# Hash-masked attention and a SiLU feed-forward: one batch's attention interleaved by hand with the feed-forward of the batch before, scores stationary, silu through tanh

## Chip, cores and metric

One core of one Trainium2 chip. The metric is device time in microseconds (us), median of several executions. Every profile is of a run in the fast state, and ratios use fast runs alone. A few single runs were in the slower state (longer, at a lower clock).

Engines are named as in the profile: PE is TensorE matmul, PEld its weight loads, ACT ScalarE, DVE VectorE, POOL GpSimd, SP SyncE, which issues transfers. "av" stands for the product of the exp'd scores with the values.

## The reference, cut to what matters

```python
# q, k, v: (4 batches, 8 heads, 768, 64);  proj: (64, 6)
q_bits = (einsum('bhsd,dk->bhsk', q, proj) > 0)          # 6 hash bits a row; the same for k
mask   = q_bucket[:, :, :, None] == k_bucket[:, :, None, :]
scores = where(mask, q @ k.T / 8, -1e9)
attn   = softmax(scores);  x = (attn @ v) -> (3072, 512)  # 8 heads side by side
h = x @ w_in                                             # (512, 2048)
out = (h * sigmoid(h)) @ w_out                           # (2048, 512), fp32
```

Both kernels put the mask into the matmul: each row carries its six bits as +-0.5 beside its 64 values. A pair of rows whose bits all agree gets the largest bit product, and any disagreement pushes exp down to nothing. Both compute the bits' products in fp32, because only their signs count.

## The kernel before

Attention for all 32 heads first, the feed-forward for all tokens last. One head, cut:

```python
for b in range(B):
    for h in range(H):
        # ... loads of q_sb, k_sb, v
        for t in range(NJ): nc.tensor.transpose(tq_ps[0:64, ...], q_sb[:, t, :], ident)   # L132, fp32
        for t in range(NJ): nc.tensor.transpose(tk_ps[0:64, ...], k_sb[:, t, :], ident)   # L135
        nc.vector.tensor_copy(out=qT32, in_=tq_ps[0:64, :])                               # L140
        nc.vector.tensor_copy(out=kT32, in_=tk_ps[0:64, :])                               # L142
        nc.scalar.mul(QT[0:64, :], qT32, QS); nc.scalar.copy(KT[0:64, :], kT32)
        # bits: fp32 projection into 6 partitions, compare, for k (L151, L153) and q (L158, L160)
        # sum of v by six matmuls (L167)
        for jt in range(NJ):
            # scores: keys stationary, 768 queries moving                                  # L179, L181
            nc.scalar.activation(out=ut, in_=st_ps, func=AF.Exp, bias=ebias, scale=ESC)    # L184
        for jt in range(NJ):
            # values and ones stationary, 768 columns of exp'd scores moving               # L194
            nc.tensor.matmul(o_ps[:, c0:c1], VV[:, jt, :], u[jt][:, c0:c1], ...)
        # copies out (L197, L199), a transfer of the sums to other partitions;
        # per two heads four reciprocals of 128x192 (L94) and two products (L100)
# then: weights cast on GpSimd, and for each 512 tokens
nc.scalar.activation(out=gt, in_=h_ps, func=AF.Sigmoid)                                    # L237
nc.vector.tensor_tensor(out=gt, in0=gt, in1=h_ps, op=ALU.mult)                             # L238
```

The softmax here doesn't subtract the row's maximum and nothing guards it: scores larger than these inputs give would overflow.

## Time and profile before

| | before |
|---|---|
| time, median of the first 3 runs | 676.81 us (675.65 to 682.14) |
| attention, up to the first feed-forward matmul | 502 us |
| feed-forward, with nothing beside it | 178 us |
| mean granted clock of TensorE, 20 to 485 us | 0.74 |
| the same, 515 to 680 us | 1.00 |
| PE, DVE, ACT busy in the span | 86%, 51%, 43% |

Read the two clocks together with the busy shares. Work at clock 0.5 takes twice as long and the engine still reads as busy. So 86% busy is not 86% of what PE can do.

### The profile page before, as it was taken

The numbers are of one execution on the slowest core, as the hardware profiler recorded it, in microseconds if no ns is written. First come the engines' busy times: TensorE is split into PE (matmuls) and PEld (weight loads), VectorE is DVE, ScalarE is ACT, GpSimd is POOL, SyncE is SP. The second block draws the span as 40 slices with busy tenths as digits, with TensorE's granted clock in tenths as the row PEclk, the third lists the DMA queues.
The fourth block names the chain that finished last, engine by engine and source line by source line (L and its number), as shares of the span: only waits on it lengthen the run. The fifth ranks groups of instructions, "written<-read, shape, count | busy, mean of one in ns | idle before, by whom it ended". The sixth has DMA issues, their size and how long they took to land.

```text
span 680.6 us, 6388 instructions
## 1 busy us (share of the span) xinstructions
PE 581.9 (86%) x2432; PEld 249.7 (37%) x2432; DVE 344.8 (51%) x363; ACT 294.3 (43%) x338; POOL 45.6 (7%) x60
## 2 busy tenths in 40 slices
PE   6997977878797977878797977979798999999996
PEld 2342433333343424333333423333333444444442
DVE  2254637384645537363754548263638345254451
ACT  2654444454455544444464545444463224133140
POOL 4422000000000000000000000000000000000000
PEclk9876767597777769676877869676779999999999
DMA  9754224042222224142222224030100100101101
GB/s 267 217 149 87 41 41 70 17 76 41 42 40 41 40 41 69 32 64 31 50 40 41 40 41 81 20 39 7 23 13 15 47 31 32 62 16 47 46 16 63
DMA packets 84271, 37.12 MB, mean 55 GB/s; under 512 B 76560, under 2 KB 76560, under 8 KB 83728
## 3 DMA queue, kind: packets, MB, share of 16 engines
q1 hardware_dynamic: 34064, 27.27, 14.3%
q0 software_dynamic: 25088, 3.15, 7.2%
q10 hardware_dynamic: 25088, 6.29, 4.5%
q8 instruction: 19, 0.31, 0.2%
q14 instruction: 12, 0.10, 0.0%
HBM read 27.26 MB, written 6.29 MB: 49 GB/s over the span
## 4 chain that ended last, share of the span: by engine, by line
PE 76%; DVE 20%; issue 3%; DMA 1%; ACT 0%; SPq 0%; DVEq 0%
PE o_ps L194 13%; PE st_ps L179 12%; PE o_ps L243 12%; PE h_ps L232 11%; PE tk_ps L151 9%; PE st_ps L181 5%; DVE KT L153 5%; DVE xT L100 4%; DVE qT L140 4%; PE tq_ps L158 4%; PE tq_ps L132 4%; DVE numpair L197 3%; PE o_ps L190 3%; DVE kT L142 2%; DVE spair L94 1%
## 5 line engine op out<-in xcount | busy, mean ns | idle before, releaser
L184 ACT ACTIVATE u<-st_ps,ebias 128x768 f16<-128x768 f32 x192 | 163.8, 901 | 141.7 <-PE st_ps L181 141.7
L179 PE MATMUL st_ps<-QT,KT 70*128 70x512 f16 x192 | 108.3, 569 | 29.8 <-DVE KT L153 29.8
L140 DVE COPY qT<-tq_ps 64x768 f32<-64x768 f32 x32 | 30.4, 950 | 142.2 <-PE tq_ps L132 141.7
L237 ACT ACTIVATE g<-h_ps 128x1024 f16<-128x1024 f32 x48 | 49.1, 1023 | 107.5 <-PE h_ps L232 107.5
L232 PE MATMUL h_ps<-xT,win 128*128 128x512 f16 x384 | 87.5, 380 | 2.6 <-DVE g L238 2.6
L243 PE MATMUL o_ps<-wout,g 128*128 128x512 f16 x384 | 87.2, 379 | 2.3 <-DVE osb L248 2.3
L94 DVE RECIPROCAL spair<-spair 128x192 f32<-128x192 f32 x64 | 79.8, 1309 | 2.2 <-DMA spair<-stmp 1.8
L181 PE MATMUL st_ps<-QT,KT 70*128 70x256 f16 x192 | 74.5, 388 | 0.0
L238 DVE TENSOR_TENSOR g<-g,h_ps 128x1024 f16<-128x1024 f16 x48 | 58.4, 1220 | 31.1 <-ACT g L237 31.1
L158 PE MATMUL tq_ps<-qT,proj 64*6 64x256 f32 (+1 forms) x128 | 51.9, 531 | 24.7 <-DVE qT L140 22.8
L151 PE MATMUL tk_ps<-kT,proj 64*6 64x256 f32 (+1 forms) x128 | 65.8, 650 | 7.6 <-DVE kT L142 7.6
L194 PE MATMUL o_ps<-u,VVo 128*128 128x512 f16 x192 | 66.5, 459 | 0.0
L147 ACT ACTIVATE QT<-qT 64x768 f16<-64x768 f32 x32 | 27.0, 842 | 75.6 <-DVE qT L140 75.6
L179 PEld LDWEIGHTS <-KT 70*128 70x128 f16 x192 | 24.1, 126 | 95.8 <-issue 92.4
L194 PE MATMUL o_ps<-u,VVe 128*128 128x512 f16 x192 | 56.4, 393 | 0.0
L243 PEld LDWEIGHTS <-g 128*128 128x128 f16 x384 | 37.3, 97 | 49.7 <-issue 6.2
L232 PEld LDWEIGHTS <-win 128*128 128x128 f16 x384 | 37.7, 98 | 48.1 <-issue 3.5
L197 DVE COPY numpair<-o_ps 64x768 f32<-64x768 f32 x32 | 30.6, 955 | 44.2 <-PE o_ps L194 43.7
L153 DVE TENSOR_SCALAR KT<-tk_ps 6x768 f16<-6x768 f32 x32 | 30.6, 955 | 34.1 <-PE tk_ps L151 34.1
L248 DVE COPY osb<-o_ps 128x512 f32<-128x512 f32 x24 | 16.6, 692 | 59.0 <-PE o_ps L243 59.0
L132 PE MATMUL tq_ps<-ident,q_sb 128*64 128x128 f32 x192 | 37.1, 311 | 5.6 <-DMA q_sb<-in_q_dram 5.6
L199 ACT COPY stmp<-o_ps 64x768 f32<-64x768 f32 x32 | 25.3, 792 | 35.7 <-DVE numpair L197 35.1
(35 smaller groups left out, 404.3 us busy)
## 6 DMA issues: line engine op xcount, KB each, us to landing
k_sb<-in_k_dram ACTq DMA_DIRECT2D x32, 192.0 KB, 3.5
q_sb<-in_q_dram SPq DMA_DIRECT2D x32, 192.0 KB, 2.6
spair<-stmp SPq DMA_DIRECT2D x32, 192.0 KB, 2.9
out_dram<-osb SPq DMA_DIRECT2D x24, 256.0 KB, 2.0
win<-in_moe_w_in_dram SPq DMA_DIRECT2D x4, 1024.0 KB, 6.7
wout<-in_moe_w_out_dram SPq DMA_DIRECT2D x16, 256.0 KB, 3.5
VVe<-in_v_dram POOLq DMA_DIRECT2D x16, 96.0 KB, 4.5
VVo<-in_v_dram POOLq DMA_DIRECT2D x16, 96.0 KB, 4.1
```

Of the source, the lines that this page charges most:

```text
L94: nc.vector.reciprocal(out=spair[:, c0:c1], in_=spair[:, c0:c1])
L132: nc.tensor.transpose(tq_ps[0:64, t * P : (t + 1) * P], q_sb[:, t, :], ident)
L151: nc.tensor.matmul(tk_ps[64:70, c0:c1], proj32, kT32[:, c0:c1], start=True, stop=True)
L153: nc.vector.tensor_scalar(out=KT[64:70, :], in0=tk_ps[64:70, :], scalar1=0.0, scalar2=0.5, op0=ALU.is_ge, op1=ALU.subtract)
L158: nc.tensor.matmul(tq_ps[64:70, c0:c1], proj32, qT32[:, c0:c1], start=True, stop=True)
L179: nc.tensor.matmul(st_ps[:, 0:512], kslice, QT[:, 0:512], start=True, stop=True)
L181: nc.tensor.matmul(st_ps[:, 512:S], kslice, QT[:, 512:S], start=True, stop=True)
L184: nc.scalar.activation(out=ut, in_=st_ps, func=AF.Exp, bias=ebias, scale=ESC)
L194: nc.tensor.matmul(o_ps[:, c0:c1], VV[:, jt, :], u[jt][:, c0:c1], start=False, stop=(jt == NJ - 1))
L232: nc.tensor.matmul(h_ps[:, c, :], w_in16[dt][:, ft * P : (ft + 1) * P], xT[dt][:, t0 : t0 + TCH], start=(dt == 0), stop=(dt == NDT - 1))
L238: nc.vector.tensor_tensor(out=gt, in0=gt, in1=h_ps, op=ALU.mult)
L243: nc.tensor.matmul(o2_ps, g_tiles[ft // 2][:, ft % 2, tt * P : (tt + 1) * P], w_out16[ft], start=(ft == 0), stop=(ft == NFT - 1))
```

## The change

Four intents: fill PE's gaps in attention with the feed-forward of the batch before; cut PE work in attention by giving each matmul more to do; take the long VectorE operations out of each head's chain; and keep one activation table loaded.

- **Order by hand.** Instructions are issued in program order. One step is one block of 128 keys of one head (192 steps); feed-forward units are handed out evenly over a batch's 48 steps.
- **Heads in pairs.** One fp32 transpose turns two heads; one projection with a block-diagonal 128x32 weight gives both heads' bits; four such projections write four groups of 32 partitions.
- **Exp'd scores stationary.** Each output has tokens on partitions and 65 columns (64 values and the sum), so normalising is a reciprocal of six elements and one product. x must then be transposed.
- **silu as h(1 + tanh(h/2))**, with the factor 0.5 taken at the output.
- **Weights** are cast while they are loaded, at the start, on the GpSimd queue.

The core of the diff, cut:

```diff
-            for t in range(NJ):
-                nc.tensor.transpose(tq_ps[0:64, t * P : (t + 1) * P], q_sb[:, t, :],
-                                    ident)
+            nc.tensor.transpose(tp[:, j * P : (j + 1) * P],
+                                src[:, t].rearrange("p h d -> p (h d)"), ident)
...
+        for c in range(4):
+            p, n = 2 * Q + c // 2, c % 2
+            nc.tensor.matmul(bp[32 * c : 32 * c + 32, 0 : c1 - c0], pw,
+                             qk32[p][:, n * S + c0 : n * S + c1],
+                             start=True, stop=True)
...
-                    nc.tensor.matmul(o_ps[:, c0:c1], VV[:, jt, :], u[jt][:, c0:c1],
-                                     start=False, stop=(jt == NJ - 1))
+        for t in range(NJ):
+            nc.tensor.matmul(o_ps[h][:, t, :], u[:, t * P : (t + 1) * P], vv[:, jt, :],
+                             start=False, stop=True,
+                             skip_group_check=True)
...
-            nc.scalar.activation(out=gt, in_=h_ps, func=AF.Sigmoid)
-            nc.vector.tensor_tensor(out=gt, in0=gt, in1=h_ps, op=ALU.mult)
+            nc.scalar.activation(out=th, in_=hp, func=AF.Tanh, scale=0.5)
+            nc.vector.scalar_tensor_tensor(out=g[ci][:, grp * f : (grp + 1) * f, :],
+                                           in0=th, scalar=1.0, in1=hp,
+                                           op0=ALU.add, op1=ALU.mult)
...
+    for s in range(NSTEP):
+        for fn in at.pop(s, []):       # transposes, casts, projections, loads planned for this step
+            fn()
+        if s % 48 == 3 and s > 48:
+            moeq.extend(moe_units(s // 48 - 1))
+        # n = units left / steps left in this batch, rounded up
+        for _ in range(n):
+            moeq.popleft()()
+        av(s)
+        if s + 2 < NSTEP:
+            score(s + 2)
```

## The prediction

> **What bounds the kernel now.** I read the busy times first, then the slices, then three stretches, then the waits and one head in order of time.
>
> ```profile
> span 680.6 us, 6388 instructions
> PE 581.9 (86%) x2432; PEld 249.7 (37%) x2432; DVE 344.8 (51%) x363; ACT 294.3 (43%) x338; POOL 45.6 (7%) x60
> PE   6997977878797977878797977979798999999996
> ...
> PEclk9876767597777769676877869676779999999999
> ```
>
> TensorE is busy 86% of the span. The slices show two regimes: about 29 slices at 6 to 9 tenths with a granted clock wandering between 0.5 and 0.9, then 11 at 9 tenths and a clock of 0.9 or more. The stretches put numbers on them (columns: the stretch, its length, busy us and count of PE, PEld, DVE, ACT, POOL, then mean granted clock, DMA share, GB/s):
>
> ```profile
> 20.00:485.00 465.00, 386.29 (x1573) 164.06 (x1572) 250.58 (x268) 229.27 (x273) 37.26 (x48) 0.74 0.30 53
> 485.00:515.00 30.00, 25.93 (x109) 11.33 (x108) 15.33 (x16) 15.75 (x17) 0.00 (x0) 0.81 0.06 14
> 515.00:680.00 165.00, 156.50 (x716) 69.56 (x713) 74.00 (x72) 42.97 (x42) 0.00 (x0) 1.00 0.11 39
> ```
>
> The first 502 us are attention: the first feed-forward matmul (L232) starts at 502.4. Less the first 15.6 us, in which the first scores are prepared, that is (502 - 16) / 32 = 15.2 us a head. The feed-forward is the last 178 us, at clock 1.00 and with nothing else beside it. In attention no engine is full; each head is a chain PE, VectorE, PE, VectorE with the clock halved for most of it:
>
> ```profile
> 211.60 1.45 PE tq_ps L158 x4
> 213.06 2.51 PE tk_ps L151 x4
> 215.57 0.02 issue
> 215.59 0.97 DVE KT L153
> 216.56 0.14 issue
> 216.69 0.58 PE st_ps L179
> 217.28 0.21 PE st_ps L181
> ```
>
> So a copy out, a fp32 projection, a compare (0.97 us on six partitions) and only then scores. ScalarE waits for scores for 141.7 us in all (L184 behind L181). VectorE can be in the way too: four reciprocals took 4.99 us in one piece at 201.97, 79.8 us in all.
>
> **What the Trainium skill says.** (1) "TensorE: Matmul & The Clock Gate", Part 1, has the clock gate at full or half rate, set by recent activity of the array. The trace agrees: the granted clock is only ever 0.5 or 1.0, and averages 0.74 in attention and 1.00 in the feed-forward. (2) "Perfetto Trace Analysis", Optimization Strategy, advises interleaving regimes whose most-contended engine differs. The stretches fit: ACT is busy 49% in attention but 26% in the last 165 us, while PE goes from gaps to 95%. (3) "ScalarE: Activation LUTs", Table sets, puts exp and tanh in one set and sigmoid in another; before there are two table loads of 1283 ns. With exp and tanh alternating 96 times, sigmoid would cost a load at each switch; tanh costs none. (4) "TensorEngine Tiling (Array Packing)", Tiling Modes, has four 128x32 tiles that can run in parallel; the new projections write four 32-partition groups. No run here shows it.
>
> **The change, part by part.** First TensorE at full clock. Costs are start-to-start times from the order of events: 512 columns 0.2155 us, 256 columns 0.108, 128 columns with its own weight load 0.055 (six L167 took 0.50 us, of which the last is 0.22), one fp32 transpose 0.109 (four L132 added 0.44 to the chain), one fp32 projection of 768 columns 1.29 (four starts, 0.43 apart for the 512 half and 0.215 for the 256).
>
> - Transposes of q and k: heads go in pairs, so 384 become 192. 41.9 us to 20.9.
> - Projections: 64 of 768 columns become 32 (two heads in one, with a block-diagonal weight). 82.6 us to 41.3 if one after the other, 10.3 if the four column groups run side by side. I take 26.
> - Sums of v on PE (192 x 0.055 = 10.6) go to GpSimd.
> - Scores: the same 192 x 0.323 = 62.
> - Attention times values: before, u moved, 192 x 0.323 plus 32 delta rows of the same size, 72.4 us. Now u is stationary and 65 columns move: 1152 pairs of weight load and short matmul. Streaming 65 columns is about 27 ns; one timed weight load began 31 ns ahead of its matmul (L179 at 107.19 and 107.22). Their sum is 58, and 55 is the closest spacing measured. I take 0.055: 63.4 us, plus 32 delta matmuls of 390 columns, 5.2.
> - New transposes of x: 96 x 0.055 = 5.3.
> - Feed-forward: the same columns, 256 x 0.2155 + 256 x 0.108 + 384 x 0.2155 = 165.6, hence 41.4 a batch.
>
> Sum before: 41.9 + 82.6 + 10.6 + 62 + 72.4 + 165.5 = 435 us at full clock. After: 20.9 + 26 + 62 + 63.4 + 5.2 + 5.3 + 165.6 = 348. So 87 us of PE work go, but the larger gain is in the other 246 us of the 681: half clock and gaps of attention.
>
> ScalarE: exps start 0.78 us apart when back to back (three in 2.48 us, each 0.90). 192 x 0.78 = 150. A tanh of 512 is about 1.023 - 512 x 0.833 ns = 0.60 us (the sigmoid of 1024 took 1.023): 96 x 0.60 = 57. Copies of 512 out of PSUM, 0.58 by the same step from L199's 0.79: 48 x 0.58 = 28. In sum 235. VectorE: the product of 1024 took 1.22, so 512 takes about 0.69: 96 x 0.69 = 66; the 24 outputs 0.69 each, 17; copies of x 16 x 0.95 = 15; normalising 32 x 0.7 = 22 (reciprocals are now of six elements); bits about 9. In sum 129. GpSimd: casts of 1536 elements at the 0.92 ns of L213, 32 x 1.42 = 45, and some 40 for v. So PE is the bound wherever the feed-forward runs beside attention.
>
> Now the time, in four stages; one step is one block of 128 keys of one head, 192 in all.
>
> - Start, 28 us. Before, the first score came at 15.6. Now the loads are twice as large, two pairs need 24 transposes (at half clock 0.22 each, 5 us), six copies, then all projections (at half clock up to 10 us), bits, and row transfers of some 3 us before a score. Then the first step waits for pair 2's q, which is issued behind those transfers and shares bandwidth with 8.4 MB of weights.
> - First batch, 48 steps without feed-forward, 52 us. PE at full clock: 0.323 + 0.33 + 0.03 + 0.11 + 0.13 + 0.03 = 0.95; ACT 0.78 + 0.15 = 0.93. Two score buffers make a ring: exp ends, av and the next score (0.65), exp again (0.90), with about 0.3 of latencies, for two steps: 0.93. Three limits within 0.02 leave little room; I take 1.08.
> - Three batches with feed-forward, 144 steps, 274 us. PE 0.95 + 41.4/48 = 1.81 to 1.83. ACT in the half with tanh 0.93 + 0.60 = 1.53, in the other half 0.93. With 4% for waits 1.90.
> - Last feed-forward alone, 41.4, plus final normalising, transposes and out transfer of about 6: 48 us.
>
> 28 + 52 + 274 + 48 = 402 us.
>
> **The rivals.** (a) **The weight loads do not hide.** A 128-column weight load lasts 97 ns in the records; if each pair took 100 ns, 1152 x 0.045 = 52 us more: 454. Against it: the loads overlap in the trace, one begins 2 ns after its predecessor's matmul. If they hide entirely, the pair takes about 30 ns: 29 us less, 373. (b) **The clock stays halved.** At the clock of attention before, 0.74, the first batch's PE need is 1.3 a step (+11 us), and the interleaved steps would take 2.5 (+85 us): about 495. For it: short gaps in each step. Against it: the feed-forward stretch held 1.00 throughout at 95% busy, and the interleaved stage should be as dense. I expect at most the first batch to suffer. (c) **A PSUM ring becomes the bound.** Three one-bank buffers serve transposes, projections, both feed-forward products and x. A hidden block needs 0.87 on PE, a wait behind an exp (up to 0.8), tanh 0.6, product 0.69, perhaps 0.3 of latencies: 3.3 us, with two steps (3.7) until its buffer comes round, and less where a transpose unit takes a turn. If that binds in the tanh half, some 0.3 x 72 = 22 us more: 424. (d) **Projections in parallel or in series**: 16 us less or 15 more. (e) **The start** could take 10 us more behind the weights' transfer.
>
> **Range and chances.** The pair cost gives -29 to +52 with the low half likelier, projections +-15, the ring 0 to +22, clock 0 to +20. Not all go one way: 374 to 438. Even with (a) and (c) together, 476, it is far below 677. Slower would take an error of 270 us. Faster 0.985, same 0.01, slower 0.005.
>
> **What would show it.** In the changed profile: PE over 90% busy and granted clock near 1.0 in the stretches of batches 2 to 4; steps of about 1.9 us there; starts of the 65-column matmuls about 55 ns apart; four projection matmuls of a unit starting together or 0.43 us apart; one table load; VectorE near 130 us and ScalarE near 235. I am wrong in the mechanism if the interleaved steps show PE waiting for tanh's product or for an exp for more than 0.2 us each, if the clock there is below 0.95, or if the first 48 steps take more than 70 us.

## The result and the profile after

The changed kernel took 380.69 us (median of 4, 377.21 to 382.31), the kernel before 676.23. The ratio is 0.562 (95% interval 0.558 to 0.566).

The page of the changed kernel, busy times and slices:

```profile
span 378.8 us, 7151 instructions
PE 329.2 (87%) x2880; PEld 193.7 (51%) x2880; DVE 127.2 (34%) x241; ACT 230.1 (61%) x337; POOL 105.9 (28%) x174
...
PE   4540578988999999999999999999999999999995
...
PEclk9955689999999999999999999999999999999999
```

PE's busy share hardly moved, 86% to 87%; what it means did. From the eleventh slice to the last but one it is at 9 tenths, with the clock at full. Stretches of the changed kernel, cut where the stages begin (same columns as in the prediction):

```profile
0.00:26.00 26.00, 11.37 (x49) 6.75 (x49) 5.88 (x27) 6.31 (x9) 16.44 (x32) 0.84 0.52 126
26.00:92.00 66.00, 45.74 (x491) 26.60 (x489) 9.94 (x23) 42.45 (x60) 27.01 (x43) 0.83 0.72 151
92.00:330.00 238.00, 227.56 (x2102) 137.17 (x2103) 88.86 (x158) 167.03 (x245) 62.45 (x100) 1.00 0.23 64
330.00:379.00 49.00, 44.48 (x242) 23.15 (x240) 22.49 (x34) 14.33 (x24) 0.00 (x0) 1.00 0.10 38
```

Three interleaved batches take 238 us at 96% PE and clock 1.00. The weak stretch is the second: a first batch of 48 steps that takes 66 us, with DMA busy 72%.

Why an interleaved step is as short as it is, in TensorE's order of events:

```profile
151.35 0.34 PE L212 MATMUL o_ps<-vv,u 128*128 128x65 f16 x6
151.53 0.49 PE L195 MATMUL s_ps<-qka 71*128 71x512 f16 x2
151.86 1.03 PE L266 MATMUL o_ps<-wout,g 128*128 128x512 f16 x4
152.73 0.35 PE L212 MATMUL o_ps<-vv,u 128*128 128x65 f16 x6
152.91 0.49 PE L195 MATMUL s_ps<-qka 71*128 71x512 f16 x2
...
155.23 1.07 PE L168 MATMUL bp_ps<-qk,pw 128*32 128x512 f32 x8
```

Starts, not durations, tell the rate: one 65-column record lasts 0.19 us here, yet the next begins 0.03 us after it began. The six pairs of weight load and 65-column matmul occupy 151.35 to 151.53, 0.18 us; scores 0.33; four feed-forward matmuls 0.87. The sum is 1.38, and none of these lines carries a wait: PE is the bound, as predicted. In the whole stretch PE is idle for 10.4 us, and 9.7 of them are waits of the first matmul of a head for the normalising of the head before. The last line is a projection unit: eight records (fp32 takes two per matmul) in 1.07 us, where four in series would start 4 x 0.86 us of work. The first four of them start within 20 ns, which the prediction named as the sign that they run side by side.

And the first batch's two long waits, in the order of events of all engines (PE's idle time and what ended it stand in brackets):

```profile
22.68 2.38 POOL L120 DMA_DIRECT2D win<-in_moe_w_in_dram  x4
...
24.51 13.75 SPq L70 DMA_DIRECT2D k_sb<-in_k_dram  x1
...
38.73 0.69 PE L136 MATMUL tp_ps<-ident,k_sb 128*128 128x128 f32 x2 [9.83 <-DMA k_sb<-in_k_dram]
...
48.64 1.12 PE L136 MATMUL tp_ps<-ident,q_sb 128*128 128x128 f32 x4 [4.50 <-DMA q_sb<-in_q_dram]
```

The weights are issued at 22.68. A load of k issued just after holds the SP queue for 13.75 us, where an earlier one took 0.83, and PE stands still. These are steps 2 and 6 of the first batch, counted from 0 (the expectations below call the first of them step 1).

| stage | predicted us | measured us |
|---|---|---|
| start, to the first av | 28 | 26.3 |
| first batch, 48 steps | 52 | 66.0 |
| three interleaved batches, 144 steps | 274 | 238.0 |
| last feed-forward and end | 48 | 48.5 |
| sum | 402 | 378.8 (span) |

DVE was busy 127.2 us (129 predicted), ACT 230.1 (235), with one table load instead of two.

### The profile page after: what moved, and what is told of

It is laid out like the page before. It is cut to its first block, busy times and chain, and to the rows that moved or that the text cites. A ratio compares the mean times of both kernels' runs of the same rounds, so it can differ in the third digit from the quotient of the medians.

```text
span 378.8 us, 7151 instructions
## 1 busy us (share of the span) xinstructions
PE 329.2 (87%) x2880; PEld 193.7 (51%) x2880; DVE 127.2 (34%) x241; ACT 230.1 (61%) x337; POOL 105.9 (28%) x174
## 4 chain that ended last, share of the span: by engine, by line
PE 71%; DVE 9%; DMA 9%; ACT 5%; SPq 3%; issue 2%; POOL 0%; ACTq 0%; POOLq 0%
PE o_ps L266 21%; PE h_ps L249 20%; PE s_ps L195 12%; DMA k_sb<-in_k_dram 9%; PE o_ps L212 8%; PE bp_ps L168 4%; DVE x_pr L222 3%; PE tp_ps L136 3%; ACT u L197 3%; PE o_ps L208 2%; DVE g L255 2%; ACT th L253 2%; DVE osb L271 1%; PE xt_ps L232 1%; SPq L70 1%
## 5 line engine op out<-in xcount | busy, mean ns | idle before, releaser
L197 ACT ACTIVATE u<-s_ps 128x768 f16<-128x768 f32 x192 | 153.8, 813 | 74.7 <-PE s_ps L195 73.8
L249 PE MATMUL h_ps<-xT,win 128*128 128x512 f16 (+1 forms) x512 | 93.9, 326 | 0.3 <-DVE xT L234 0.3
L255 DVE SCALAR_TENSOR_TENSOR g<-th,h_ps 128x512 f16<-128x512 f32 x96 | 66.1, 688 | 58.2 <-ACT th L253 58.2
L212 PEld LDWEIGHTS <-u 128*128 128x128 f16 x1152 | 60.0, 99 | 40.7 <-ACT u L197 13.4
L143 POOL TENSOR_SCALAR qka<-qk 64x1536 f16<-64x1536 f32 x16 | 23.5, 1466 | 170.7 <-ACT qk L138 170.7
L212 PE MATMUL o_ps<-vv,u 128*128 128x65 f16 x1152 | 68.1, 196 | 3.5 <-ACT u L197 3.1
L253 ACT ACTIVATE th<-h_ps 128x512 f32<-128x512 f32 x96 | 57.3, 597 | 22.5 <-PE h_ps L249 20.1
L195 PE MATMUL s_ps<-qka 71*128 71x512 f16 x192 | 48.8, 337 | 4.3 <-POOL vsb L156 4.3
L195 PE MATMUL s_ps<-qkb 128*128 128x512 f16 x192 | 48.0, 332 | 0.0
L138 ACT COPY qk<-tp_ps 128x512 f32<-128x512 f32 x48 | 28.2, 587 | 26.7 <-PE tp_ps L136 26.7
L136 PE MATMUL tp_ps<-ident,k_sb 128*128 128x128 f32 x96 | 17.6, 302 | 10.5 <-DMA k_sb<-in_k_dram 10.4
L143 POOL TENSOR_SCALAR qkb<-qk 64x1536 f16<-64x1536 f32 x16 | 23.5, 1471 | 1.2
```

What stands on the lines that cost most here:

```text
L136: nc.tensor.transpose(tp[:, j * P : (j + 1) * P], src[:, t].rearrange("p h d -> p (h d)"), ident)
L138: nc.scalar.copy(qk32[p][:, 512 * i : 512 * (i + 1)], tp)
L143: nc.gpsimd.tensor_scalar(out=dst[rows, :], in0=qk32[p][rows, :], scalar1=CS, scalar2=1.0, op0=ALU.mult, op1=ALU.mult)
L195: nc.tensor.matmul(sp[:, c0:c1], ks, t[rows, c0:c1], start=True, stop=True)
L197: nc.scalar.activation(out=u, in_=sp, func=AF.Exp, scale=ESC)
L212: nc.tensor.matmul(o_ps[h][:, t, :], u[:, t * P : (t + 1) * P], vv[:, jt, :], start=False, stop=True, skip_group_check=True)
```

## The experiments

Stage times in this section are starts of av matmuls in the traces. The changed kernel itself was not run again, so differences from its 380.69 us are also differences between calls; the stage times in the traces are what carries them. In the last two calls the kernel before spread from 672.92 to 689.41 us, and the measuring program gives all four verdicts there as unclear.

### Feed-forward last

```diff
-        if s % 48 == 3 and s > 48:
-            moeq.extend(moe_units(s // 48 - 1))
...
-    for u in moe_units(B - 1):
-        u()
+    for b in range(B):
+        for u in moe_units(b):
+            u()
```

(and four buffers instead of two for the x tiles)

> All feed-forward after all of attention, nothing else changed (the x tiles get four buffers instead of two). Theory A, most of the gain is the rewritten attention itself and interleaving only fills what PE leaves idle in it: the 144 later steps take the 1.03 us that undisturbed steps of the first batch took in the changed kernel, the feed-forward 4 x 41.4 us, so 26 + 66 + 148 + 166 + 7 = 413 us, clock 1.0 in attention. Theory B, interleaving is what keeps the clock up: without it attention runs at about half clock, 1.45 us a step, about 475 us.

Measured: 407.65 us (ratio 0.603), correct. Attention without feed-forward, 92 to 236 us, as a stretch of this kernel:

```profile
92.00:236.00 144.00, 122.14 (x1473) 68.98 (x1470) 31.66 (x73) 123.10 (x176) 62.28 (x100) 1.00 0.29 75
```

Theory A holds, B falls: the clock is 1.00 without interleaving, and a step takes 0.99 us. Of the 296 us that the change takes off, interleaving is worth 27; the rest of the rewrite brings about 269. In the traces attention ends at 234 us instead of 502, and the feed-forward takes 170 us instead of 178. The reason why interleaving brings so little is in the same line: PE is 85% busy there, so a batch's 41.4 us of feed-forward finds little room. A batch takes 47.4 us without and 81.6 with it; about 7 us are hidden.

### Late weights, early loads, both

Late weights:

```diff
-    load_weights()
...
+    for i in range(8):
+        plan(11 + 5 * i, lambda i=i: load_weight(i))
```

> The eight weight transfers are issued one by one at steps 11, 16, ... 46 instead of all before step 0. Theory W, the two waits of 10 and 5 us for k and q of pairs 2 and 3 come from the 8.4 MB of weights on the same DMA engines: they shrink to under 2 us each and the whole takes 363 us (17 less), with no wait at step 51. Theory O, they come from the order of issue on the SP queue (behind eight row transfers of bits): the waits stay and the time stays at 380.

Early loads:

```diff
     load_v(0)
     load_v(1)
+    load_qk(2)
+    load_qk(3)
...
     v_unit(1)
-    load_qk(2)
-    load_qk(3)
```

> q and k of pairs 2 and 3 are loaded ahead of the bits' row transfers; the weights are left where they were. Theory O (order of issue): the waits at steps 1 and 6 vanish, 363 us. Theory W (weights' bandwidth): these four loads now finish before the weights start, so the waits at steps 1 and 6 vanish here too, but bits of the first four heads and v of later pairs come later; 363 to 368. So this run alone does not tell O from W; with the run of late weights it does, and it shows whether order alone is a remedy.

> Late weights and early loads together. If each removes the same wait: as the better of the two alone, 361 to 363 us. If a wait of 4 us before the first av (its transposes wait for q of pair 2) goes as well: 358.

Measured: late weights 362.88 us (0.537), early loads 372.12 (0.550), both 363.14 (0.537), all correct. With late weights and the order of the other loads untouched, no step of the first batch is longer than 1.9 us, and its stretch is 49 us instead of 66:

```profile
25.00:74.00 49.00, 42.77 (x500) 24.68 (x498) 9.93 (x23) 42.22 (x61) 30.19 (x48) 0.97 0.85 180
```

So theory W: it was the weights' traffic. Early loads alone remove these two waits as expected, but uncover another, of 7.2 us at step 22, which the expectation of 363 to 368 missed. The next k load is stuck on the SP queue until 52.95, while the last of the weights lands at 52.36, and the transfers that bring the bits to their rows stand in line behind it:

```profile
47.18 5.77 SPq L70 DMA_DIRECT2D k_sb<-in_k_dram  x1
53.05 0.75 SPq L178 DMA_DIRECT2D qka<-bits  x1
...
56.58 0.80 PE L195 MATMUL s_ps<-qka 71*128 71x512 f16 x2 [7.21 <-DMA qka<-bits]
```

Both together gain nothing over late weights: the first av comes at 26.2 us instead of 24.8, because the early loads now stand ahead of the first rows of bits (the first of these is issued at 19.55 us instead of 13.63, and PE waits 9.53 us for it).

### Every av matmul twice

```diff
-        for t in range(NJ):
+        for t in list(range(NJ)) * 2:
             nc.tensor.matmul(o_ps[h][:, t, :], u[:, t * P : (t + 1) * P], vv[:, jt, :],
```

> Every 65-column matmul with its weight load is issued twice (numerator and denominator both double, so the output is right but for the delta term of 1e-8). Theory S, a pair costs the 29 ns by which starts lie apart in the records: 144 steps that PE bounds take 6 x 0.029 = 0.174 us more each, 25 us, and the first batch, bound by a ring through ScalarE, 0 to 8: 405 to 413 us. Theory L, a pair costs 55 ns as predicted and the records mislead: 0.33 a step, 48 to 63 us more: 428 to 443.

Measured: 409.37 us (0.601), correct: 28.7 us more than the changed kernel. An interleaved batch takes 89.3 us instead of 81.6, which is 0.027 us for each added pair. Twelve pairs now stand where six stood, and the scores start 0.36 us after them instead of 0.18:

```profile
162.31 0.52 PE L212 MATMUL o_ps<-vv,u 128*128 128x65 f16 x12
162.67 0.49 PE L195 MATMUL s_ps<-qka 71*128 71x512 f16 x2
```

Theory S holds: starts 29 ns apart are the true cost, and the predicted 55 was too high.

### Projections in series, alone and with late weights

```diff
-            nc.tensor.matmul(bp[32 * c : 32 * c + 32, 0 : c1 - c0], pw,
+            nc.tensor.matmul(bp[:, 0 : c1 - c0], pw[:, c, :],
                              qk32[p][:, n * S + c0 : n * S + c1],
-                             start=True, stop=True)
+                             start=(c == 0), stop=(c == 3))
```

(and the weight is filled as four blocks of 128 columns, with eight small transfers instead of two)

> The four projections of a unit use all 128 columns, each with weights that are zero outside its own 32, and accumulate, so that none can run beside another; the sums are the same. Theory P, the four column groups ran side by side (a unit of 512 columns took about 1.0 us in the changed kernel, against 4 x 0.86 in series): per two units 4 x 1.29 - 1.65 = 3.5 us more, seven times in the loop and once before it: 28 us, 404 to 409. Rival, the chain hides it or it was never parallel: under 5 us more.

Measured: 414.22 us (0.608), correct: 33.5 us more than the changed kernel. Each later pair of units costs 3.4 us more (88.4 against 81.6 us for a batch with two), as theory P has it. A unit of 512 columns now takes 3.60 us:

```profile
131.11 3.60 PE L169 MATMUL bp_ps<-qk,pw 128*128 128x512 f32 x8
```

The total is over its 404 to 409 because of the start: the first av moves from 26.3 to 49.7 us, of which the first batch gives 6.8 back. This needed a run of its own:

> Serial projections and late weights together. The serial projections alone cost 33.5 us, of which the trace puts 16.7 into the start and the first batch. Theory Q: most of that start is not projection work but the loads of q and k falling behind the weights (they were issued 7 us later); with late weights only the projection work remains, 7 x 3.4 us in the loop plus about 4 at the start: 391 us, 28 over late weights alone. Rival: the start pays for the projections themselves, 33 us over late weights: 396 or more.

Measured: 394.75 us (0.583), correct: 31.9 us over late weights alone, between Q's 28 and the rival's 33, nearer the rival in sum. The traces of the two runs divide it. In the batches the difference is 23.5 us, as Q had it (7 x 3.4). The first av is at 33.7 us, 8.9 later than with late weights alone, where Q allowed 4. Of these 8.9, about 3.6 are the projections: their first matmul starts 5.0 us later (15.65 against 10.70), and the first transfer of bits that follows them 8.6 later (22.20 against 13.63). The 5.0 us come before any projection: six more small transfers stand on the SP queue ahead of the second pair's loads, and its q is issued at 8.55 us instead of 4.67. So they belong to how this experiment fills its weight, which neither theory had counted, and not to serial projections. The other 14.5 of the 23 us of shift at the start went away when the weights came late.

### Sigmoid instead of tanh

```diff
-            nc.scalar.activation(out=th, in_=hp, func=AF.Tanh, scale=0.5)
+            nc.scalar.activation(out=th, in_=hp, func=AF.Sigmoid)
...
-                                           in0=th, scalar=1.0, in1=hp,
-                                           op0=ALU.add, op1=ALU.mult)
+                                           in0=th, scalar=1.0, in1=hp,
+                                           op0=ALU.mult, op1=ALU.mult)
```

(and the factor 1.0 at the output)

> silu as h times sigmoid(h), as in the kernel before, in place of tanh. The build has some 128 table loads instead of one. Theory T, tanh was needed for the interleave to pay: each load takes 1.28 us of ScalarE, two per step in the half of each batch with hidden blocks, less the slack of about 0.4 us a step: 63 x (2.56 - 0.4) = 135 us more, 515 us. Rival, the loads hide behind PE: under 10 us more.

Measured: 535.98 us (0.786), correct: 155 us more. ScalarE in its order of events:

```profile
120.91 1.28 ACT L253 ACT_TABLE_LOAD   x1
122.20 0.60 ACT L253 ACTIVATE th<-h_ps 128x512 f32<-128x512 f32 x1
122.82 1.28 ACT L197 ACT_TABLE_LOAD   x1
124.11 0.81 ACT L197 ACTIVATE u<-s_ps 128x768 f16<-128x768 f32 x1
```

128 loads of 1.283 us make 164 us; most of it lands on the path (an interleaved batch takes 132.7 us instead of 81.6). The run is 21 us over the estimate; the mean clock of this run fell from 0.96 to 0.83, which fits PE now waiting in each step, but the two were not separated. Tanh is what makes this interleaving pay: with sigmoid it costs far more than the 27 us it brings. An order that groups the sigmoids, to switch less often, was not tried.

### What attention before was made of

Three kernels leave work out of the kernel before: bits set to a constant (no projections, no compares), no reciprocals, and neither.

```diff
-            for c0, c1 in ((0, 512), (512, S)):
-                nc.tensor.matmul(tk_ps[64:70, c0:c1], proj32, kT32[:, c0:c1],
-                                 start=True, stop=True)
-            nc.vector.tensor_scalar(out=KT[64:70, :], in0=tk_ps[64:70, :],
-                                    scalar1=0.0, scalar2=0.5,
-                                    op0=ALU.is_ge, op1=ALU.subtract)
+            nc.gpsimd.memset(KT[64:70, :], 0.5)      # the same for q
```

```diff
-                    nc.vector.reciprocal(out=spair[:, c0:c1], in_=spair[:, c0:c1])
+                pass
```

> The kernel before without its projections and compares: the six bit rows are set to a constant, so the result is wrong on purpose. Theory C, the chain of projection, compare, projection, compare at a halved clock is the largest part of a head's 15.2 us: 1.45 + 2.51 + 0.97 + part of the second compare lie on the path, 4 to 5.5 us a head, 130 to 175 us less: 500 to 545 us. Rival, the heads are bound by the amount of PE work and the rest of VectorE's work (reciprocals, copies) takes the place: under 80 us less.

> The kernel before without its 64 reciprocals of 1.31 us (it multiplies by the sums instead, so the result is wrong on purpose). Theory C2, they lie beside the scores and are hardly on the path (the chain shows them at 1%, 7 us): 650 to 670 us. Rival, VectorE in order holds up the next head's copies: up to 80 us less, 596 to 640.

> The kernel before without projections and compares and without reciprocals (wrong on purpose). Alone, the first omission took 85 us and the second 60. If they shorten different parts of each head's chain they add up: 530 to 540 us. If both only uncover the same remaining chain (copy out, scaling, scores, av), clearly less than the sum: 560 or more. If the shorter gaps also raise the clock in attention above 0.80: below 520.

Measured: without bits 595.72 us (ratio to before 0.874), without reciprocals 618.66 (0.913), without either 555.89 (0.819). The last includes one slow run; the fast ones have 554.48. Against the fast runs of before that is 84, 59 and 123 us less. The results are wrong, so only times are read from these three.

The first lies outside both expectations, 130 to 175 or under 80: the projection chain was on the path, but less of it than I had counted, and by the waits in the trace others took part of its place (the L157 sums of v now wait 58.9 us for a ScalarE copy, before 21.8). The GpSimd fills that stand in for the bits cost waits of their own, 3.4 us in 14 small ones and one of 6.0. The second went against my theory: I had read 1% for the reciprocals in the chain and concluded that they cost little. VectorE's order of events in the kernel before shows what they do:

```profile
201.97 4.99 DVE L94 RECIPROCAL spair<-spair 128x192 f32<-128x192 f32 x4
207.78 0.95 DVE L197 COPY numpair<-o_ps 64x768 f32<-64x768 f32 x1 [0.83 <-PE o_ps L194]
208.66 1.91 DVE L100 TENSOR_TENSOR xT<-numpair,spair 64x768 f16<-64x768 f32 x2
210.60 0.95 DVE L140 COPY qT<-tq_ps 64x768 f32<-64x768 f32 x1
```

and the kernel without them:

```profile
205.66 0.95 DVE L99 TENSOR_TENSOR xT<-numpair,spair 64x768 f16<-64x768 f32 x1
213.63 0.95 DVE L139 COPY qT<-tq_ps 64x768 f32<-64x768 f32 x1 [7.01 <-PE tq_ps L131]
```

The reciprocals themselves lie beside the scores. In the kernel before, two products (L100) stand behind them and behind the copy L197, where the next head's copy out (L140) must wait for them. In the kernel without, one product per head stands right after the compares and the small L169, is done early, and the copy waits only for PE.

That this comes from the length of the reciprocals is not shown. In 15 of the 16 pairs of heads VectorE is idle for 0.83 to 3.60 us between the last reciprocal and L197, waiting for PE; the products come only after L197, although what they read has been written by then. So what delays them is their place in VectorE's order, and that order differs between the two kernels as built: two products per pair after L197 in one, one per head before it in the other. The run took out the reciprocals and changed the order at once. Reciprocals kept, with the products ahead of L197, was not tried, so how the 59 us divide stays open.

Without either, 123 us go, against 143 for the two omissions added: between the two outcomes of the expectation, with about 20 us that both take. The granted clock between 20 and 380 us is still 0.76, and a head still takes about (380 - 16) / 32 = 11.4 us, against 5.9 in the run with the feed-forward last. What makes up that remainder was not separated.

### A faster version

On top of late weights: the loads of pairs 2 and 3 go between the row transfers that the first score needs and the rest; the first planned transposes start at step 4; at the first step of a head the next scores go ahead of av.

```diff
+                if Q == 0 and c == 2:
+                    load_qk(2)
+                    load_qk(3)
...
-    load_qk(2)
-    load_qk(3)
...
+            ts = s0 + 2 * i if Q > 1 else (4, 6, 7, 9, 10, 11)[i]
...
+        if s % NJ == 0 and s + 2 < NSTEP:
+            score(s + 2)
         av(s)
-        if s + 2 < NSTEP:
+        if s % NJ and s + 2 < NSTEP:
             score(s + 2)
```

> Late weights, plus three moves meant to take away waits that the profiles name: the first quad's loads of pairs 2 and 3 go between the row transfers that the first score needs and the others, the transposes of pairs 2 and 3 start at step 4 instead of 0, and at the first step of each head the next scores go ahead of av, so that the normalising of the head before has more time. If each wait is what ends last where it stands: start 5 us less, 8 head changes of 0.3 us in the first batch and some in the later ones: 352 to 356 us against 363. If they only uncover another wait: 360 to 363.

Measured: 352.74 us (350.46 to 356.60; fast runs alone 352.15; ratio 0.520), correct, against 362.88 (361.86 to 363.92) for late weights. It ran on another chip, whose runs of the kernel before spread as said above, so the traces weigh more than the difference of medians: first av at 21.5 us instead of 24.8, an interleaved batch 79.7 us instead of 81.6. It beats both kernels. The three moves were not run separately, but the first two act only up to step 11, so the traces divide the gain: 3.3 us at the start and 0.6 in the first batch, and 5.9 in the three interleaved batches, where only the third move acts. There PE's waits for normalising fall from 9.7 us to 4.0.

## Why the prediction was right

The prediction was 402 us, 374 to 438. It came true by the named mechanism; the sizes of three terms were off and partly cancelled (36 us too much in the interleaved batches, 14 too little in the first), so part of the closeness is luck.

- **PE is the bound in the interleaved steps: right.** 96% busy, clock 1.00, and the starts of a step without extras add up to 1.38 us with nothing between. None of the three signs of a wrong mechanism came, though one was near: PE never waits for tanh's product there and for an exp in only two of the 144 steps (0.8 us in all), the clock is 1.00, and the first 48 steps take 66 us, not over 70.
- **The pair of weight load and 65-column matmul: 55 ns predicted, 29 measured**, and confirmed by doubling it. I had added the load to the stream; it hides. The 55 that seemed to confirm the sum was misread: in L167 128 columns stream behind a load of one column, so it is the time of 128 columns, and the changed kernel's transposes of x, 128 columns with a 128-column load each, start 55 ns apart too. In 144 steps the term shrinks from 0.33 to 0.176 us a step, 22 us in all. Rival (a) in its cheap form was the true one.
- **Projections: 26 us taken, about 13 measured.** The column groups run side by side (a unit of 512 about 1.0 us, one of 256 about 0.6; eight of each). In the interleaved batches there are only five pairs of units, 8 us, where 0.13 a step made 19. Transposes there are 13 us, not 16, for the same reason. With the pair, that is the whole 36 us by which 274 was too high; the 4% for waits was about right.
- **First batch: 52 predicted, 66 measured.** Undisturbed it takes 49 (late weights). The step that failed is the bandwidth shared with the weights: I put its effect into the start, at step 0, and gave rival (e) 10 us; it came at steps 2 and 6, and late weights take 17.8 us off.
- **Start and end: right** within 2 us.
- **The clock (b): right** that interleaved steps hold full clock, and they are not needed for it: attention alone holds it too, in the run with the feed-forward last, at PE 85% busy. What lowered the clock in the kernel before was not tested.
- **The PSUM ring (c), three accumulator buffers coming round: not seen as a bound**, although a tanh step with extras can take 2.5 us; the traces give these steps to PE's own work or to a head's normalising (9.7 us over 18 waits in the interleaved batches), which the prediction did not list among the waits.
- **Where the gain comes from: not split.** I called gaps and half clock of attention the larger gain, which is true, but did not say how much of it interleaving would bring. My own terms imply 5 us: without interleaving the 144 later steps would take 144 x 1.08 = 155.5, the feed-forward 165.6 and the end 6, in sum 327, against 274 + 48 = 322. It brings 27. The rest of the rewrite brings about 269, of which, by estimate, 130 us are PE work at full clock (435 to 348 predicted, less 30 and 13 for the two terms above, makes 305).
- **The reading of item (2), interleave where the most-contended engine differs, did not fit.** PE was the busiest engine in both stretches (386 of 465 us and 156.5 of 165), so the feed-forward could only go into PE's own gaps.

## What to carry to other kernels

Interleaving two stages pays only what the bound engine leaves idle in the first: measure that stage with its chain repaired before counting on the other to fill it. Taking an operation out can save far more than its share of the chain of waits (59 us against the 7 read there); look at what stands behind it in its engine's order, and check whether that order changed with it. A large prefetch issued early can starve the small loads that the next steps need; spread it over the steps that have no use for it yet.

## What the Trainium skill lacked or had wrong

- "TensorE: Matmul & The Clock Gate", Back-to-back issue gap, says that in a stream of weight loads and matmuls the spacing is about 81 ns at 128 columns and 131 at 512, and that the isolated formula N/2.4 + 2.5 misses this. Here, with a 128-column load before each matmul, 65 columns start mostly 29 to 30 ns apart (the formula gives 29.6), 128 columns 55 (L232), and 512 columns 215.5.
- "ScalarE: Activation LUTs", What ACT_TABLE_LOAD costs, has 2.66 us for each switch, 1.28 of load and 1.38 of drain. In the sigmoid run the load takes 1.283 us and the activation starts within 20 ns of its end; a switch costs 1.3 us.
- "TensorEngine Tiling (Array Packing)", Tiling Modes, gives column tiles without a figure for fp32. Here four 128x32 fp32 projections of 512 columns took about 1.0 us against 3.4 to 3.6 in series.
- "VectorE: DVE Perf Modes" describes how a reciprocal is computed but gives no duration. Here 128x192 fp32 took 1309 ns and 128x6 took 192, so some 6 ns an element after a fixed part; copies out of PSUM took 955 ns for 768 elements and 692 for 512, about 1 ns an element.
- "DMA: Bandwidth & Descriptors", Issuing engines are not separate DMA queues, says that transfers from all queues share the 16 engines and interleave; it gives no figure for how long a small load is held up by a large one on another queue. Here a 384 KB load held its queue for 13.75 us behind the weights' transfers, against 0.83 before them.
